# Thresholded attention and a maxout feed-forward on one core: another written order, other PSUM slots and other masks

## The chip, the core and the metric

The kernel runs on one core of a Trainium2 chip. The engines are TensorE (PE in the profile; PEld is its loading of weights), VectorE (DVE), ScalarE (ACT), GpSimd (POOL) and SyncE (SP), which here only issues transfers. Each takes its instructions strictly in the order in which they were written and waits on semaphores for the others. The metric is the device time of one execution in microseconds (us).

## The reference

```python
def _attn_ref(q, k, v, tau):                      # 8 batches, 8 heads, 576 positions, 64 wide
    scale = 1.0 / np.sqrt(q.shape[-1])
    scores = scale * np.matmul(q, k.transpose(0, 1, 3, 2))
    thresh = np.max(scores, axis=-1, keepdims=True) - tau
    scores = np.where(scores >= thresh, scores, -1000000000.0)
    scores = scores - np.max(scores, axis=-1, keepdims=True)
    attn = np.exp(scores)
    attn = attn / (np.sum(attn, axis=-1, keepdims=True) + 1e-09)
    return np.matmul(attn, v).astype(np.float32)

def _moe_ref(x, w1, w2, w3, w_out):               # 4608 tokens, 512 wide, 768 inside
    h = np.maximum(np.maximum(x @ w1, x @ w2), x @ w3)
    return (h @ w_out).astype(np.float32)
```

The heads of the first function, side by side, are the rows x of the second. All inputs and the output are float32.

## The kernel before

The work is cut into 16 quads: four heads of one batch. A quad has nine chunks, each with 128 rows of queries for two heads, so a chunk has two halves of scores, 128 x 576 each; there are 144 chunks and 288 halves. Two quads make a batch. When a batch's two quads are through, its feed-forward can run: 18 pieces that make the hidden rows (three weights by six blocks of 128) and then the output pieces.

A half goes through these steps. TensorE makes its scores in a PSUM slot (a bank of 1024 columns; there are four slots, 0 to 3). VectorE copies them to an SBUF tile z and takes the row's largest value on the way (`maximum`, line by line in the print below). ScalarE and VectorE then make the numerators and their sum. VectorE takes the reciprocals of a chunk's two sums, GpSimd multiplies them in (tile P, bfloat16), and SP turns P by a transposing transfer into the quad's tile ptq. Once all nine chunks of a quad are turned, TensorE multiplies them with v (two products to a quad), and ScalarE or VectorE evacuates the result to the feed-forward's input xt.

How a half's numerators are made is told by its digit in `MASKED`:

- 0, plain: VectorE computes a threshold th from the largest value, ScalarE applies a Prelu to z with it (values under the threshold become huge), and ScalarE takes the exponential and its sum.
- 1, masked: ScalarE takes the exponential of z, VectorE compares it with the smallest admitted numerator, multiplies and sums, in one instruction that reads z twice. There is no threshold and no second pass on ScalarE.
- 2, direct: as 0, but ScalarE reads the scores from the PSUM slot, not from z, and needs no separate threshold. The slot is free only when ScalarE has read it, and not already when VectorE has.
- 3: direct and masked.

Ahead of a quad's scores come transposes of its q and k on TensorE (T), which ScalarE and VectorE evacuate (tiles qt, kt) and of which GpSimd makes a copy with the halves of partitions swapped (qs). The weights come in twelve pieces through a staging tile and are cast to bfloat16 on GpSimd. 38 warming matmuls stand at the start.

What sets the order is the string `ORDER`: one letter for each step, read from left to right, and each step writes its instructions at the end of its engines' queues. S, T, O, F and N put work on TensorE into the PSUM slot whose digit follows (scores, transposes, product with v, feed-forward piece, last ninth of the output rows), and B is the second half of the oldest open F. The letters that follow them:

- m, s, e, n, k: a half's first pass on VectorE, its threshold, its first pass on ScalarE, its exponential on ScalarE (unmasked) or its masking on VectorE (masked)
- r, p, t: a chunk's reciprocals, the normalising of one half on GpSimd, the transposing transfer on SP
- a, c, q, y: evacuation of turned q and of turned k, the swapped copy, the cast of v
- h, v, u, w, x, j, f: evacuations of feed-forward pieces, output pieces and products
- l, g, z, o, i, d: a load of q, k or v, a load of weights, its cast, and the stores

All transfers stand in one queue, SP's, but for three at the start and two at the end, which ScalarE's queue issues.

Of the kernel before, what the change touches and what calls it, by code (L numbers as in the profile page):

```python
# [45 lines left out]
nyrrsmyBepT1svS0hpcT2nS3zmaS1erpgsF2mntpsBmnS3yvF1etssT0myeBprS2cnpS3mnS0ympelF2epF3lmBnzslssvS0htBrqmeS2vpn
S1gF0sepmF3teqBmF2erssvpBtnBkphF0eS1vtS3znmF2nrBmqteS1rpvBnS3pmlnF0pmgeS1qsBsrhmS3pevS2npS1mF0npsO3ermpesmO2
zewepgsskBxtT3nF1vS2nklBarS0mlphS3mtepF2sS1rmnyBmetF3pvT0eBpcnS2tzT1nvS0asmzS3temS2qeS1meF0trkpmS3lenpBmnlys
reklpF1umerpskS3upBeoketmS0uS2umpS3tesmS1qeT0myO2nqlrsnlprcO3etqsmepwS0xptS1mnF3psnmS2BlerskpS1thF0meF3pmeBF
2ktnBveBsrS1nvpS0hmyF3emF2npBrssT0eprtvBaF1kS3nqvBeF0myhyS2kyleF3mBelBvnpS2snsS0vptemS1pnF3rmpT2tnBmpeF0scS1  # L50
htBrnmpF3erT2rpvlBasS1pstvnS2pmeF0pS3emtBqnmT2S1hcqS3empF2eS0rsqmtS1epsmBeF3pmnF0stsvBeBknF2klhF1BvelS0nrvpB
emT3pS2arvS0ptnS3mpnO1smtesrkpeF2swnlrpmeT0S1qtescS3epBmnpmnT0trskS3paS1umS0ulqmeS3lmyS1nopS2smelS0rmeS3psmn
O1ypersmqO2etkpemO0lewqxlknpS3tS1keF2momS3lexF0ktT1enkBercpnsBpumN1ertkphkF3jS0rursS1empBnmF2ptS0vpS1smeF3yt
BsnsmBpnvS0pT1hmF2atT3srepS0cF1eprBsmeqF3vnByBynvplS2nsS0plmhS1mteS2mF0nF3mteS1rrspBnmS2pelvBlepF1smT0leqBvl
aS2rkhF3oqnsS0mtS1epmBeqsF2ssmtS0epvBeyF1mnF3vpBesrS0ktphBermS1npT2svO0nytmpncT3eS1wF2nrmS0aBrsmnqF3vnT1pS0c
eBptsF2mhpS1eS3pmteS0qmBeO1spmnkteF3rvnpT0BsskapS2xvS0erS1qmtnS3pmnF2mqlespmeS1rtkBepresmT3puS1cuS0ptmnS3pS2
meyS1lrekpF0tnsmempO3lekteskO2nrsmpeBkpxrnwS1uptS3muS2pnmF0yoeS1mF3lesymBtnS2srkpS1hmBeF0spveF2ertBmpT3nrsvS
1paBlmpnS0tS3qhmF1epsmS2leBymF3tevF0nBknlS1rsvpS2esmqnBF3srmhpS1epS0tmeF2pssBrempBtesvS0ynF1mT3lnpBvF0lhsrcS
2tnT1mBnF3valS2nrBsqmeF0pvS1epS2meBptsmS3eqF1hmT2peBcS3tnskT2O0arkplnmO2lerpvewptS3xkpS1nF2meF0sstreBsmpS3nv
pBnmS1tS2hmT3eF0rmpnF1cBpnBrevptT3S2apvS0qmtS3S1enmqF2esrsqmiepmleS0soykeS1plBnmemtS3ukS0uT1snrlO2cpekynO1me  # L60
ymeF3pwxskteS0keS1BrrnkopmF2pmS0BqeuurtsmF1phS3srnpS2meT0ptBmeS3ykpaN2esvempF0tS1jkpF3ermBeS2ptvnS1pmBnS0rls
hsmpS2elF3mqntS1mpF0nsrBskpeF2lsmBetBpveF1yhvS3lnkS2lesF0mytnBmBerqsS3veF2lpvnF1pBsmT0htBceF3rT2vnpBsaS0pvnF
1qmtS2nBsrnmT0pS3hrcpF2esS1mpteS0rmpS3emBpntF1svqnS0ssBmpeoT2vO3lamtneF1wS0nrlBpmeS3qsrS2hsmS0pnmF1eptS3smeB
pmF2ntS0veS3rsmnpS1BnpO0veytrempS2empS3xsmS1tekF0nsknlT2rmpBelmlpnscS3quS1umyS2eorT0kpeO3tmeyO1ewlepsmF3etka
rknS2qklT0nBmxespcS2eryF0mpF1uskpuBtnS2BhmqF3nsvS0peS2srmtpF1eBmpeF0srvnBptS2hyS3pmeF1lmeBlBevtF3nkT2S0arrvp
BnS2mphS1smpF0ntS3smnpBmeF1lsT2esvlF3nrBrcptBnvpS2eS0qmlhS1tsnprsmT3F2epmS0aptBemF3yevS1oS0nqmBnpsrS2mnF1ptv
S0epmBeS3mthS2skeF0F1snmlBeklO3ersvpnrmByepF0swT2eqtBvnqF3ssrcS1hpiBmpT0S2vaptS1snmS0pnT3mqF2tecT1BarmS3pnS1
vqeS0mF2pesrmnptmS3npT1seS0qctBeymqermpS1eS3mpuF0nmtuskS1eS2klnS3smBesrsepO1upmemO2txrkpukeO3wnkpS0xS2emF3et
rmS1pnBssspmF2hS0rtepS3mnBpmF1etS0veF3mnN2rnpBpjF0evtF2esBkBkhF1nsvS3eBmBevO3hrkS2pwnS1mnF3prmS2eptsF0mnBpsS
1sevyS2terBmpeF3svS1iyepBmoS0yhmtF2ekF3nBsmS1ersBvpnF0pmeF2BvteS1hBmF3rsS0vpeF1rknpBBmnO2vhptO0xrpnS3pwS2trm  # L70
# [759 lines left out]
```

## Time and profile before

| | |
|---|---|
| median of 3 runs | 446.71 us (445.96 to 448.13) |
| span of the profiled execution | 444.8 us, from its first to its last instruction |
| granted TensorE clock over the span | 0.988 |
| transfers | 88.50 MB, 199 GB/s over the span |
| HBM read and written | 35.65 MB and 9.44 MB |

The profile is of one execution. Its times count from the first instruction of the span; what lies around the span (the run's time minus it) is in the runs' times alone. All instructions go through one recording helper, so nearly all rows name line 93, and rows are told apart by their tiles: sc are scores, tp transposes, ph and po the two parts of the feed-forward, o the products, z the halves, ptq the turned P.

### The profile page before, as it was taken

How to read it: one execution, taken by the hardware profiler on the slowest of the kernel's cores; microseconds unless marked ns; L12 is line 12 of the kernel's file. 1: busy time of each engine (PE TensorE's matmuls, PEld its weight loads, DVE VectorE, ACT ScalarE, POOL GpSimd, SP SyncE). 2: the span in 40 equal slices, each digit the busy share in tenths (PEclk: the TensorE clock that was granted, in tenths of full speed). 3: DMA queues.
4: the chain of work that ended last, by engine and by line, in shares of the span. 5: the costliest groups of instructions: out<-in, count | busy, mean ns of one | idle time of the engine just before them, and what ended most of it. 6: DMA issues, size and time to landing. Idle time of an engine off the chain costs nothing.

```text
span 444.8 us, 14254 instructions
## 1 busy us (share of the span) xinstructions
PE 422.4 (95%) x5188; PEld 320.2 (72%) x5190; DVE 392.8 (88%) x1228; ACT 403.0 (91%) x836; POOL 311.9 (70%) x420
## 2 busy tenths in 40 slices
PE   7767789999999999999999999999999999999996
PEld 6334347787788767787788777788688886787873
DVE  3887999999999999999999999998999998899642
ACT  3999999999999999999999999899999999987632
POOL 2799989997878687696785877676676685457400
PEclk8998999999999999999999999999999999999999
DMA  7999999999999999699899999989999977487633
GB/s 188 275 293 199 291 169 269 235 243 262 229 180 194 212 222 292 125 256 167 143 234 189 230 198 203 209 168 210 208 206 194 244 151 105 83 179 136 145 116 108
DMA packets 213959, 88.50 MB, mean 199 GB/s; under 512 B 189184, under 2 KB 202240, under 8 KB 213888
## 3 DMA queue, kind: packets, MB, share of 16 engines
q1 hardware_dynamic: 213360, 86.96, 95.9%
q8 instruction: 41, 0.67, 0.6%
q10 hardware_dynamic: 528, 0.62, 0.5%
q14 instruction: 30, 0.25, 0.2%
HBM read 35.65 MB, written 9.44 MB: 101 GB/s over the span
## 4 chain that ended last, share of the span: by engine, by line
PE 86%; ACT 5%; DVE 4%; issue 2%; DMA 1%; SPq 0%; DVEq 0%; ACTq 0%
PE ph L93 32%; PE sc L93 32%; PE po L93 10%; PE o L93 9%; ACT z L93 5%; PE tp L93 3%; DVE z L93 3%; DMA qm<-in_q_dram 1%; ACT qt L93 1%; SPq L93 0%; DVE xt L93 0%; DVE hm L93 0%; DVE stage L93 0%; DVE rs L93 0%; ACT ob L93 0%
## 5 line engine op out<-in xcount | busy, mean ns | idle before, releaser
L93 POOL TENSOR_SCALAR P<-z,rs 128x576 bf16<-128x576 f32 x250 | 200.6, 814 | 63.3 <-DVE rs L93 28.1
L93 DVE TENSOR_SCALAR_CACHE_REDUCE z<-sc 128x576 f32<-128x576 f32 x250 | 183.7, 750 | 14.8 <-PE sc L93 10.1
L93 PE MATMUL sc<-kt,qs 64*128 64x256 f32 (+2 forms) x640 | 182.6, 423 | 5.7 <-DVE z L93 2.3
L93 PE MATMUL sc<-kt,qt 64*128 64x320 f32 (+2 forms) x640 | 182.4, 433 | 5.2 <-ACT z L93 3.3
L93 PE MATMUL ph<-xt,w 64*128 64x288 bf16 (+2 forms) x2160 | 170.8, 283 | 0.1
L93 PEld LDWEIGHTS <-w 64*128 64x128 bf16 (+1 forms) x2160 | 130.1, 94 | 28.6 <-issue 4.3
L93 ACT ACTIVATE z<-z 128x576 f32<-128x576 f32 x174 | 117.6, 679 | 0.1
L93 PEld LDWEIGHTS sc<-kt,qs 64*128 64x128 f32 (+1 forms) x640 | 92.4, 180 | 25.7 <-DVE z L93 5.7
L93 ACT ACTIVATE z<-z,th 128x576 f32<-128x576 f32 x143 | 106.2, 769 | 5.0 <-DVE th L93 4.2
L93 PEld LDWEIGHTS sc<-kt,qt 64*128 64x128 f32 (+1 forms) x640 | 91.9, 179 | 19.7 <-ACT z L93 5.9
L93 DVE SCALAR_TENSOR_TENSOR z<-z 128x576 f32<-128x576 f32 x76 | 62.2, 830 | 0.5 <-ACT z L93 0.5
L93 PE MATMUL po<-wo,hT 64*128 64x512 bf16 (+3 forms) x454 | 53.5, 354 | 0.3
L93 POOL COPY qs<-qt 64x640 f32<-64x640 f32 (+3 forms) x66 | 43.0, 652 | 10.8 <-ACT qt L93 7.2
L93 ACT ACTIVATE z<-z,nm 128x576 f32<-128x576 f32 x68 | 50.6, 767 | 0.0
L93 DVE TENSOR_TENSOR hm<-ph,hm 128x576 bf16<-128x576 f32 (+2 forms) x54 | 37.0, 686 | 9.2 <-PE ph L93 8.9
L93 ACT ACTIVATE hm<-ph 128x576 bf16<-128x576 f32 (+2 forms) x54 | 31.8, 589 | 13.4 <-PE ph L93 12.8
L93 POOL TENSOR_SCALAR P<-stage,rs 128x576 bf16<-128x576 f32 x38 | 30.4, 804 | 19.3 <-ACT z L93 5.4
L93 PEld LDWEIGHTS <-hT 64*128 64x128 bf16 (+2 forms) x456 | 30.0, 95 | 16.5 <-issue 2.3
L93 DVE TENSOR_TENSOR hT<-ph,hm 128x576 bf16<-128x576 f32 (+2 forms) x54 | 37.0, 686 | 4.0 <-PE ph L93 2.3
L93 PE MATMUL o<-ptq,vb 128*64 128x64 bf16 (+2 forms) x544 | 39.0, 281 | 0.0
L93 ACT ACTIVATION_READ_ACCUMULATOR z<-z 128x1 f32 x174 | 34.3, 197 | 0.0
L93 PEld LDWEIGHTS <-vb 128*64 128x64 bf16 x544 | 23.3, 111 | 12.8 <-issue 4.9
(45 smaller groups left out, 431.6 us busy)
## 6 DMA issues: line engine op xcount, KB each, us to landing
vm<-in_v_dram SPq DMA_DIRECT2D x32, 256.0 KB, 4.8
qm<-in_q_dram SPq DMA_DIRECT2D x15, 512.0 KB, 5.0
km<-in_k_dram SPq DMA_DIRECT2D x15, 512.0 KB, 5.3
out_dram<-ob SPq DMA_DIRECT2D x14, 512.0 KB, 4.0
stage<-in_moe_w_dram SPq DMA_DIRECT2D x9, 512.0 KB, 5.2
ptq<-P SPq DMA_TRANSPOSE x144, 4.0
vr<-in_v_dram SPq DMA_DIRECT2D x16, 128.0 KB, 3.4
stage<-in_moe_w_out_dram SPq DMA_DIRECT2D x3, 512.0 KB, 4.9
```

Source lines behind the costliest of these rows:

```text
L93: ins = fn(*a, **kw)
```

## The change

Two constants are replaced, `MASKED` and `ORDER`. No function, tile or pool differs. The 288 digits differ in 115 places; the string has 3481 characters where it had 3465, because it has 16 thresholds (s) more, and four n became k. All else in it occurs as often as before, at other places and with other slot digits.

```diff
 MASKED = """
-232222322322222222021032222202332122123122200200111000000000100000000011
-000010111020011000101000000001100001001000010011111100000000100100000000
-110010030111000100010000000001010100001110001011010100110000000000000000
-100101101011000000120000001010000000110011100000001110001000010011111021
+320220312002220000101010000320210002020210010010301000000010100000001101
+001001011010101100001000000000110000101010001111011000100000100010000000
+110001001110100100010000001000111000000100011011101000011000010000010000
+010101000111000100100000000101000000011110001110101000000000101000011121
 """
...
 ORDER = """
-llllllglllT0laclT1laclzllqqS0qqS1meS2mS3lmlT0enlkS1ylmlT2eamelrnpS3leqlmnyS1qcapS0emtnrcS3pmnT2qmepgrelS1qya
-gS0pmelT2mqnS3tcpemqS2nlkT1eytaS0rmnT1kpermS3yS2enczrmS1qT0enmepnqtS3nprmaymgpeS0lptS2mppT0mtpS1enencnqsS3re
...
+lllllllllT1lcaqqlT2S3agcqqmlS2S0elmlkeT1lmnS2lscS0aelrmS3plmeqmlqnS2zeslS1mT3nlpS0maygecreqekpS2nmnpT3meyskS
+2qaetqT0mnS1yrcnplT2rsmpS0elS3rpamemqnT1tpS2eclpnmS1persS2mnpS0tsmS1eqgmeqsnszS3nrT0mtpemlS1paS2smepT0mnqS1t
...
 """
```

The digits by kind, over all 288 halves and over the first 36 and the second 36:

| | plain (0) | masked (1) | direct (2) | both (3) |
|---|---|---|---|---|
| all, before | 169 | 78 | 33 | 8 |
| all, now | 185 | 86 | 13 | 4 |
| halves 1 to 36, before | 3 | 2 | 25 | 6 |
| halves 1 to 36, now | 18 | 5 | 10 | 3 |
| halves 37 to 72, before | 22 | 8 | 5 | 1 |
| halves 37 to 72, now | 24 | 9 | 2 | 1 |

SP at the very start of the program; stage is the staging tile of the weights, the other tiles are loads of q, k and v (q_147 and k_149 hold the ninth column of rows). Before:

```order
L93 DMA q_147<-in_q_dram 64x2x64
L93 DMA qm<-in_q_dram 64x512 x2
L93 DMA stage<-in_moe_w_dram 128x4x256
L93 DMA k_149<-in_k_dram 64x2x64
L93 DMA q_147<-in_q_dram 64x2x64
L93 DMA km<-in_k_dram 64x2x512
L93 DMA qm<-in_q_dram 64x2x512
L93 DMA vm<-in_v_dram 64x4x256 x2
```

Now:

```order
L93 DMA q_147<-in_q_dram 64x2x64
L93 DMA qm<-in_q_dram 64x512 x2
L93 DMA k_149<-in_k_dram 64x2x64
L93 DMA q_147<-in_q_dram 64x2x64
L93 DMA km<-in_k_dram 64x2x512
L93 DMA qm<-in_q_dram 64x2x512
L93 DMA vm<-in_v_dram 64x4x256
L93 DMA stage<-in_moe_w_dram 128x4x256
```

The first piece of the weights moved behind the other half of the first quad's q and k and half of its v.

ScalarE in the first quad; z<-sc,nm is a direct first pass, z<-z,th a plain one, z<-z,nm a masked one, z,sm<-z the exponential with its sum. Before:

```order
L93 ACTIVATE qt<-tp 128x2x320
L93 ACTIVATE z<-sc,nm 128x576 x2
L93 ACTIVATE z,sm<-z 128x576
L93 ACTIVATE z<-sc,nm 128x576
L93 ACTIVATE z,sm<-z 128x576 x2
L93 ACTIVATE z<-z,th 128x576
L93 ACTIVATE z<-sc,nm 128x576
L93 ACTIVATE z,sm<-z 128x576 x2
L93 ACTIVATE z<-z,nm 128x576
```

Now:

```order
L93 ACTIVATE z<-z,th 128x576 x2
L93 ACTIVATE z,sm<-z 128x576 x2
L93 ACTIVATE z<-z,th 128x576
L93 ACTIVATE qt<-tp 128x2x320
L93 ACTIVATE z<-z,th 128x576
L93 ACTIVATE z,sm<-z 128x576
L93 ACTIVATE z<-z,nm 128x576
L93 ACTIVATE z<-z,th 128x576
L93 ACTIVATE z,sm<-z 128x576
L93 ACTIVATE qt<-tp 128x2x256
```

Direct passes became plain ones, which wait for a threshold of VectorE, and the second evacuation of a turned q stands nearer to the first.

TensorE between the second and the third product of the first batch (the third is the first of the second quad; its instructions are o<-ptq). Before, from the stretch's first transposes to its last:

```order
L93 MATMUL tp<-identf,km 128x64 x8
L93 MATMUL tp<-identf,k_277 128x64 x2
L93 MATMUL sc<-kt,qs 128x320
L93 MATMUL sc<-kt,qt 128x256
L93 MATMUL sc<-kt,qs 128x256
L93 MATMUL sc<-kt,qt 128x320
L93 MATMUL tp<-identf,qm 128x64 x8
L93 MATMUL sc<-kt,qs 128x320
L93 MATMUL sc<-kt,qt 128x256 x2
L93 MATMUL sc<-kt,qs 128x320
L93 MATMUL tp<-identf,km 128x64 x8
L93 MATMUL sc<-kt,qt 128x320
```

Now, from the stretch's beginning:

```order
L93 MATMUL tp<-identf,km 128x64 x8
L93 MATMUL tp<-identf,k_305 128x64 x2
L93 MATMUL sc<-kt,qt 128x320
L93 MATMUL sc<-kt,qs 128x256
L93 MATMUL sc<-kt,qs 64x256 x2
L93 MATMUL sc<-kt,qt 64x320 x2
L93 MATMUL tp<-identf,qm 128x64 x8
L93 MATMUL sc<-kt,qt 64x320 x2
L93 MATMUL sc<-kt,qs 64x256 x2
L93 MATMUL sc<-kt,qs 128x256
L93 MATMUL sc<-kt,qt 128x320
```

Of the three groups of transposes there two are left; the third stands behind the products. In the whole stretch there are nine halves of scores, before and now.

Further on, SP's order differs in how far loads run ahead of the turned P: ahead of the 94th transposing transfer stand 83 of the 104 loads before and 93 now, and ahead of the 40th 49 and 51.

More of the change, by code (lines that the diff above doesn't have):

```diff
@@ L46 @@
[L46 to L70, printed above, removed]
@@ L71 @@
-npS0mnF3pmteF1pBeBvtS0rS2vpS3empF1ktkF0kBereskpemBkperumO2uptO3xpN1wtenkO2jrF3pxF1hpF2nvF3tvF1rhF2pvF3pvF1hF
-2tvF3vF1hF2voF3vF1ohF2vF3vF1hF2vO3vO1wF2xuuF1oF0hiF3vF1vF0hF3vF1vF0hF3vF1vF0hF3vF1vF0hF3vF1vF0huF3vF1ovF3uoF
-0uoN1fjdi
+lllllllllT1lcaqqlT2S3agcqqmlS2S0elmlkeT1lmnS2lscS0aelrmS3plmeqmlqnS2zeslS1mT3nlpS0maygecreqekpS2nmnpT3meyskS
+2qaetqT0mnS1yrcnplT2rsmpS0elS3rpamemqnT1tpS2eclpnmS1persS2mnpS0tsmS1eqgmeqsnszS3nrT0mtpemlS1paS2smepT0mnqS1t
+eT3rcplemqS0nS2tymanskS0yeS3srpetS1pnmgpekS2eqtsmnynrmpS0esklzT3emlnrcpnsrtS3permgpemepmtS0nzslnS1pmepkS2emt
@@ new lines @@
+nS0plmnresmpS2erspsS0mtepO3mleqklnT0perwntS2pnlS1zmasmepS0teS3qmnS2qrstnrS1mpeO3pnmtpemT2nprsS0ceytS1mnkpT0x
+stmeS3plesrS2mgpeS1slmpangkS2nrmS0petrmpS1emS3pelmO0qnsmpnO1serkpewS3etkS2qxT0lmnF1zsceF3smBepS0rkhpBemT2tS1
+apvS0nmqF3nF2trmyBzngssBveT0pS1shrcgpS3nmT2peF0mtpS1arseT2myS3pecF1nymBtnS2vpnS3rsmpS0etsmpBeF2mzntF3vBeyS0k
+yhgBrempS1nsF2vtpF0esmlBqesBrlvqnS3klF1phS2mleF0prsnsmBpS3tevBpnmF2nqS1vS3ezrmBnF0mptS1hsrspBlemS3gpevS2yeS1
+mF0tnmpO3nkzesmO2esrwpeBgkpxT3vF1aS2rkepBtmnS3lpsS0hmF2eqmS1eBytsrmyF3nzlvT0eT1cBpnS2tvpaS0nsrzmS1etmS3peS2m
@@ new lines @@
+pF0tskeqemF1nsrmpetBkpnkS3tukS2lumBelymlrS0rsuplS2umyS3lepmS1oepT0smO2nqmntyrO3cqelkpelwS0xS1pssmeF3pemS2F0n
+rmpBeskS1phBktF2evF3eBmnBvS0thrsS1kpnlF3mnlF2prBsmeByevtT0F1lavpS3eBpmnS2sF0srshmpF3ekBpnBtvnS2qrvS0eprmF3et
+S1mqnBlsmpT2hF0srcpeS1tyF3emplBnspT2vBapS1ssnvS2qemF0tqS3emBynmT2tS1hrcpS3empS0ntsF2melS1mF3nsBrmpntF0vpeBos
+BkeF2khF1tnsBveS0rvptBnmT3pS2avS0esqrmO1erpmteT3pwnS0pcF2epmntS3keT1lsS0rnmpBemptarskqS3usS1meS0ptmuS3nqmS1e
+lmpS2elS0srmpS3nlmpO1eosmqelO2kyxemO1nwterkpT0eS3ceF2pmnykyS0estrBkpxkelF1rmluS3pulskBnyN0lemhkS2ptjF3sermS1
@@ new lines @@
+peBmF2pnvS0npS1rsmBnptmF3eT0ssvBatS1khF2qlemS0BerrpmT1epF3svtF0nsqcBeS2pvnBtpmeS1oyrS3mhpS2nmptF1nsmS0pleBrm
+pF3nvS2teT0sslmF1eBkaBnsrqvS2hS0qmeF3ptmS1nBpsmnF2prevS0F1ptessmBpeBsvtF3hkS0lnBrmpleS1vT2peO0mnlscnT3lrwS1p
+aF2mepS0treBpmF3nvyT1qnBcS0hpF2srempS1teS3mqBnkS0ptnO1smemteF3rvxlT0BskaS2evqS1npmS0tnysS3meF2smpermqeT0S1sc
+pnBrmtepkyS0uS3muyS1epmS2lnF0pmoermpelS3skpO2elklnkO1elswnrmByxektpS1usrS3umS2peF0mpeS1mBynpsmtF3hS2srknpBtm
+eS1F0pveF2sntmBnT3rvpS1atBpmeS0yrS3shmqtS1essF2mpeF0kqnF3smBetBrpvnlBprevS1lphS2lmnS0pmF3eptrS1mnBpmnF0ptsS2
@@ new lines @@
+veBosmeF1svT3nBtrecpS2hF0pmtnF3skBeT1srvS2paBtemqF0lnvS1pS2emBqermS3pnF1smT2eBchS3lskeT2O0lkakeqO2mtnsqlvS3x
+wpS1nsrF2mpeF0rmpBestS3pevByemS1hS2tmpT3nF0rsmpnF1cBpeBtveT3S2rnvpS0astmpS1nmyS3eyF2smqnrstmepS1lnqS0mBelpsm
+elkT1uS0ceS3lmeO1rknpiO0ewpumtnF1kelkxS2lkeS3sBrmepntpmF0uorS2rpuBnmyS3hsF1tmepT2lBkapS0essvS3eN2pmtnrmpF0ek
+pS1jtBrnmF3lpnvS2opS1smeS0mBetS2mhS1ersmpF3tnF0kpBemF2sBrsevpBkF1qhtvS3nS2srpnrmBpeS0mF3pnmF2yteBvpeT0svqF1e
+tBsscF3hkBnT2vS0aBemlqS2nvpF0nT1rmpBesS3cphF2rsmtpeS1rS0pnmS3teqBmF1epsvS0ntpsBmelT2ymO3evntrspF1welS0kaBnmS
@@ new lines @@
+3qS2hmpS0nrsF1mqeS3smpF2eBtrsmpnBvnpS0sS3epmS1etrvO0pelmekS2yxtmS3eF0mnpmnyT1yssrkS2npBemtpeclS3urS2pmuS1nsm
+T0tO3akoeqO2elwpnlkT0eyrF3cximeqlS0snpBmeptskS1uF0mnBsurkpF1hrS2eBpmteS0pvF3lnS2prmeBpstF1mnF0peslvBkS2hS3rm
+peBtrF1epsmT2npvBtaF3kpS0nsvBtemqS2ohS1rymnpF0sS3metpBemT2nF1rscpF3evBtqnBsvpS2hsrS0pemS1npmF2temT3S0assBnmF
+3tnvS1S0ermpBemS2peF1svS0nmBerS3mpthS2kF0pnF1smeBrempO3nsvpteskF2qnBwBnrvtpT0eF3srscqS1hBepmT0S2vaS1smnqT3S0
+mtnqF2secT1yBparmS3eqvS1eS0mpeF2mpempT3nS1ctqnS0smBermtnpS3kepS1muF0usrskpeS3meS2tpmeS1oBknmemnO3kuurO2kyxeO
@@ L74 @@
+1wetpsnkpS0xS2meF1rmnS3pBrsptmS0hF2pemS3perF1smBptnsS0vpeF3ktN2emeskBjF0rnvptBersS2pohBpF1evpF3nmBtnBkO0hsvt
+eS2wrS1nrpmF3npsmS2eBpsmF1npvS0eytS2rsymBnpF3veipS0mBS1mhtF2nrsF3mpeBstpS1evF0emBeBvtS1hsF2nmS3nF0rsmpF1ekBp
+nBvBesvO2hO3rkxpntS1rweS0pmF3nmpS2F1spremBpteBvpS0eS2vtS3mF1metkeF0mnnBrkpekBukurO1upoO2xpO1wprN3xptuF2jpF1h
+F0tvF3vF1hF2vtF0vF1hF2vF0ovF1hF3vF2ivF1hF0vF2vF3hF0vO2vO3wF1xF0uF2hF3voF0vF2hF3vF1vF0hF2vF1vF0hF2vF1vF3hF2vF
+0vF1hF2vF0vF2uF1ouN2ofjdi
 """
```

3 lines of the change are left out of this document (removed).

## The prediction

> **What bounds the kernel now.** I read the page's busy shares first, then the chain of waits, then a table of busy time cut at every 36th first pass over a half of scores (the kernel does 288 of them, two to a chunk of 128 queries).
>
> ```profile
> span 444.8 us, 14254 instructions
> PE 422.4 (95%) x5188; PEld 320.2 (72%) x5190; DVE 392.8 (88%) x1228; ACT 403.0 (91%) x836; POOL 311.9 (70%) x420
> ...
> PE 86%; ACT 5%; DVE 4%; issue 2%; DMA 1%; SPq 0%; DVEq 0%; ACTq 0%
> ```
>
> ```profile
> core 0: us, PE busy (x) PEld busy (x) DVE busy (x) ACT busy (x) POOL busy (x), PEclk, DMA share, GB/s
> 8.90:53.30 44.40, 33.11 (x254) 18.74 (x252) 36.90 (x112) 42.14 (x93) 39.27 (x54) 0.90 1.14 264
> 53.30:99.00 45.70, 43.00 (x538) 31.65 (x540) 44.84 (x142) 45.45 (x96) 41.63 (x55) 1.00 1.11 230
> 99.00:148.00 49.00, 49.00 (x649) 39.87 (x647) 46.99 (x151) 48.79 (x101) 40.07 (x53) 1.00 1.13 217
> 148.00:201.50 53.50, 53.41 (x711) 40.23 (x706) 51.04 (x165) 52.16 (x108) 39.37 (x52) 1.00 1.04 221
> 201.50:250.60 49.10, 49.10 (x641) 38.24 (x637) 46.56 (x152) 47.98 (x100) 36.34 (x49) 1.00 1.05 190
> 250.60:305.30 54.70, 53.70 (x714) 42.62 (x709) 52.08 (x161) 52.14 (x109) 39.35 (x53) 1.00 1.00 199
> ```
>
> TensorE is idle for 444.8 - 422.4 = 22.4 us. The table says where: 11.3 us between 8.9 and 53.3, 2.7 us up to 99, then almost nothing but 1.0 us in the sixth row. The rest lies before 8.9 and in the store that ends the program. So from about 70 us on the end is the sum of TensorE's work, and both orders do the same work. In the first row ScalarE sets the pace (42.14 of 44.40); in the second ScalarE and VectorE both do (45.45 and 44.84 of 45.70). What TensorE gets done early is fixed by the order: the third product of the first batch stands behind the 52nd score half in both versions. A gain or loss is therefore a shift of that point, or a new stall behind it.
>
> **The change part by part.** Masks first. I count four kinds of half: plain (0), masked (1), direct (2), direct and masked (3). Direct falls from 41 to 17, masked rises from 86 to 90, plain from 169 to 185.
>
> ```profile
> L93 ACT ACTIVATE z<-z,th 128x576 f32<-128x576 f32 x143 | 106.2, 769 | 5.0 <-DVE th L93 4.2 <-DVE rs L93 0.4
> L93 ACT ACTIVATE z<-sc,nm 128x576 f32<-128x576 f32 x39 | 28.3, 746 | 2.9 <-DVE z L93 2.9
> L93 ACT ACTIVATE z<-z 128x576 f32<-128x576 f32 x174 | 117.6, 679 | 0.1
> L93 ACT ACTIVATION_READ_ACCUMULATOR z<-z 128x1 f32 x174 | 34.3, 197 | 0.0
> L93 DVE TENSOR_SCALAR th<-nm 128x1 f32<-128x1 f32 x169 | 22.7, 144 | 0.2
> L93 DVE SCALAR_TENSOR_TENSOR z<-z 128x576 f32<-128x576 f32 x76 | 62.2, 830 | 0.5 <-ACT z L93 0.5
> L93 DVE DVE_READ_ACCUMULATOR z<-z 128x1 f32 x76 | 6.1, 80 | 0.0
> L93 ACT ACTIVATE qt<-tp 128x640 f32<-128x640 f32 (+3 forms) x34 | 21.0, 618 | 4.5 <-PE tp L93 4.3
> ```
>
> A half that stops being direct costs ScalarE 769 - 746 = 23 ns, and VectorE a threshold of 0.144 us if it is plain. A masked half costs VectorE 0.83 + 0.08 = 0.91 us and spares ScalarE its exponential of 0.68 + 0.20 = 0.88 us. By blocks of 36 halves VectorE gains 15 thresholds = 2.2 us in the first, 2 thresholds and one masked half = 1.2 us in the second, then 0.1, 1.5 (two masked more, two thresholds fewer), 0.8 and 0.8 us. Against this stand its idle times in the table: 7.5, 0.9, 2.0, 2.5, 2.5 and 2.6 us. So I cost the first block and blocks three to six at nothing (VectorE's idle time hides them; without it they cost their 2.2 and 3.2 us), and the second at 1.2 - 0.9 = 0.3 us. Bounds: 0 and 1.2.
>
> The same stretch on ScalarE, up to the numerators of the second quad's last half: 38 exponents, 28 exponentials in both, 14 of the exponents direct where 32 were, and 9 evacuations of a transposed q where 8 were. That is 18 x 0.023 + 0.618 = 1.0 us more on the engine that sets the pace there. Bounds: 0 (if it hides in the 2.3 us that ScalarE idles) and 1.0.
>
> The start. SP now issues the first weight behind the first eight q, k and v loads, no longer ahead of the second half of q and k.
>
> ```profile
> 11.93 0.24 PE L93 MATMUL tp<-identf,qm 64*128 64x64 f32 x1 [0.48 <-DMA qm<-in_q_dram]
> 10.80 0.74 ACT L93 ACTIVATE z<-sc,nm 128x576 f32<-128x576 f32 x1 [0.39 <-DVE z L93]
> ```
>
> That q load is what ended TensorE's 0.48 us. ScalarE is nearly dense from 10.80 on, whoever waits for q, so at most 0.48 + 0.39 = 0.9 us comes back, at least nothing; I take 0.4 us, its own wait.
>
> The point where TensorE becomes dense. The last turned P of the second quad is issued at 65.4 and lands 3.5 us later, at 68.9; the product starts at 69.39.
>
> ```profile
> L93 SPq DMA_TRANSPOSE ptq<-P x1: 1504/1504/1504, 65.4 to 65.4; - x1
> ...
> DMA to landing us min/median/max: 3.5/3.5/3.5
> ```
>
> ```profile
> 69.39 1.18 PE L93 MATMUL o<-ptq,vb 128*64 128x512 bf16 x16
> ```
>
> ```profile
> 58.03 0.46 PE L93 MATMUL tp<-identf,qm 64*128 64x64 f32 x8 [0.64 <-DVE z L93]
> ```
>
> With +1.0 and -0.4 us the landing moves to 69.5. Between the second and third product TensorE has nine score halves as before, but two groups of transposes where it had three, so it would be ready 0.46 us sooner and stands until the landing. The start is 0.1 us later and the group is still to be done: 0.1 + 0.46 = 0.6 us. Bounds: -0.9 (the whole start gain, if the score halves ahead come sooner with it) and 0.5 + 0.46 = 1.0 (no start gain).
>
> The same look at the other late products:
>
> ```profile
> L93 SPq DMA_TRANSPOSE ptq<-P x1: 1398/1398/1398, 160.8 to 160.8; - x1
> ...
> DMA to landing us min/median/max: 3.4/3.4/3.4
> ```
>
> ```profile
> 164.42 1.18 PE L93 MATMUL o<-ptq,vb 128*64 128x512 bf16 x16
> ```
>
> The sixth quad's last P lands at 164.2, 0.2 us ahead of its product. Behind the last normalisation the new order leaves TensorE one group of transposes less before that product: 0.46 - 0.2 = 0.3 us of wait. Bounds: 0 and 0.5. The new order leaves more work there before the fourteenth quad's product and less before the tenth's and the twelfth's, but no product waited for a P in this trace; I take nothing there, with 0.5 us as the bound.
>
> Loads and stores. From the 40th turned P to about the 115th, SP issues up to ten loads earlier than it did.
>
> ```profile
> POOL vb L93 <- DMA vm<-in_v_dram: 3.2, 2, 2.6
> ...
> PE tp L93 <- DMA qm<-in_q_dram: 2.2, 3, 1.4
> ```
>
> No load after the first 12 us ended a wait of TensorE; GpSimd's 3.2 us lie on an engine idle 133 us. So earlier loads earn nothing in an execution like this one; if they had not been covered, the cost would have been these few us. A turned P now stands in SP's queue behind loads that it used to precede.
>
> ```profile
> 280.59 0.58 SPq L93 DMA_DIRECT2D km<-in_k_dram  x1
> ```
>
> ```profile
> SPq L93 <- POOL P L93: 130.9, 83, 6.0
> ```
>
> Each such load takes SP 0.58 us, but SP stands 130.9 us for P alone, which covers ten of them; I take nothing, with 0.58 us per turned P as the bound. The end is TensorE's alone: after the last scores come 33 us of matmuls without a gap, so softmax that ends sooner there earns nothing.
>
> ```profile
> 407.04 5.39 PE L93 MATMUL po<-wo,hT 64*128 64x512 bf16 x48
> ...
> 435.67 4.82 PE L93 MATMUL po<-wo,hT 128*128 128x512 bf16 x29
> ```
>
>
> One stall is left, and it shows what a masked half can do:
>
> ```profile
> 276.94 1.46 POOL L93 TENSOR_SCALAR P<-z,rs 128x576 bf16<-128x576 f32 x2
> ...
> 277.13 2.60 DVE L93 SCALAR_TENSOR_TENSOR z<-z 128x576 f32<-128x576 f32 x1
> ...
> 280.52 0.48 PE L93 MATMUL sc<-kt,qs 64*128 64x256 f32 x1 [0.94 <-DVE hm L93]
> ```
>
> ```profile
> L93 DVE SCALAR_TENSOR_TENSOR z<-z x76: 736/750/2601, 11.6 to 414.2; 128x576 f32<-128x576 f32 x76
> ```
>
> An operation with a median of 0.75 us took 2.60 while GpSimd normalised two halves of P in a row, and TensorE stood 0.94 us. That is one of 86 masked halves; with 90 I expect it again elsewhere, so 0. Bounds: -0.9 and +0.9. The Trainium skill, "SBUF — State Buffer", section "Who interferes with whom", says that a VectorE instruction with two SBUF inputs and a GpSimd instruction that reads SBUF exclude each other for a whole instruction, which speaks against each further masked half. The row agrees that it is held up, but by more than one GpSimd instruction. By that rule four more such instructions, each behind one normalisation, would add four normalisations to VectorE; by the mean of the row above they add a tenth of that, and the sum goes by the mean.
>
> Sum: 0.3 + 0.6 + 0.3 = 1.2 us on the span of 444.8. The median of the runs is 446.71, 1.9 us over that span; I carry this over: 446.71 + 1.2 = **447.9 us**.
>
> **The rivals.**
>
> VectorE becomes the bound: slower. The added 0.1 + 1.5 + 0.8 + 0.8 us of blocks three to six stop hiding, and the second block costs its full 1.2. It decides once VectorE has under about 1 us idle in a block, as it has in the second; the fourth would keep 1.0. Price: 3.2 + 0.9 = 4.1 us more, if half of it reaches TensorE 2.0: 450 to 452. For it: both engines at 95% to 98%, and the 0.94 us stall behind one long masked operation. Against: ScalarE is relieved in the same blocks by 0.88 us for each masked half, and so far TensorE stood still for almost none of VectorE's waits after 70 us.
>
> The change doesn't do what it says: slower too.
>
> ```profile
> DMA to landing us min/median/max: 3.2/4.0/8.1
> ```
>
> A turned P that lands in 8.1 us where 4.0 is the median is 4.1 late, and the tight products have 0.2 to 0.5 us. The new order is no looser there: from the last normalisation to the product it has no more work on TensorE for the second and sixth quads and less for the tenth and twelfth. One such landing costs 3.6 us: 451.5. For it: the three times shown differ by 2.2 us. Against: this profile holds the 8.1 and has no such stall.
>
> The head gains: faster. Direct halves keep a PSUM slot until ScalarE has read it, and TensorE waited for that:
>
> ```profile
> PE sc L93 <- ACT z L93: 4.0, 9, 0.7
> ...
> PE tp L93 <- ACT z L93: 2.9, 2, 2.1
> ```
>
> With 18 of 31 direct halves gone from the first block, these 6.9 us shrink, and ScalarE is fed sooner. It can win no more than its own idle time in the first row, 2.3 us; with the stall at 280 gone too that is 3.2: 443.5. Against: TensorE isn't the bound there, so most of its waiting moves only to another place.
>
> **How the numbers follow.** The forecast has 0.52; VectorE 0.22; a late landing 0.10; the head 0.16. By the bounds of its terms the forecast alone runs from 446.7 - 0.9 - 0.9 = 444.9 to 446.7 + 1.2 + 1.0 + 0.5 + 0.5 + 0.9 = 450.8. Half a per cent, 2.2 us, is about what a measurement of this kernel can tell from no change; 0.06 of the forecast's chance lies beyond it, past 448.9. So faster 0.16, same 0.46, slower 0.06 + 0.22 + 0.10 = 0.38. The range takes in the slower cases as far as 452 and the head's case down to 444.2; what is left out is most of that case and a tenth of the slower ones.
>
> **What would show it.** The first two rows of the table: if ScalarE's busy time up to the second quad's last landing grows by about 1 us and that product starts near 69.5 us plus or minus 0.5, the head is as I say; a start before 68.5 would be the third rival. VectorE's idle time in the second and fourth blocks, and TensorE's waits that it ends after 70 us, decide the first rival: under 1 us in all, it has fallen. A TensorE wait ended by a turned P in front of a product would be the second. If TensorE's busy time itself differs by more than 1 us, the premise of equal work is wrong, and with it the sum.

## The result, and the profile after

The changed kernel takes 443.85 us (median of 6 runs, 442.66 to 444.25), the kernel before 446.50 us (6 runs, 445.68 to 448.44): a ratio of 0.9939, 95% interval 0.9921 to 0.9958. It is 2.7 us faster. The forecast was 1.2 us slower.

The page of the changed kernel, with the span, the busy shares, the chain of waits, and the group of masking instructions:

```profile
span 442.0 us, 14289 instructions
PE 420.4 (95%) x5188; PEld 318.1 (72%) x5190; DVE 398.2 (90%) x1252; ACT 402.3 (91%) x828; POOL 319.5 (72%) x420
PE 84%; DVE 6%; ACT 5%; issue 2%; POOL 1%; DVEq 0%; POOLq 0%; ACTq 0%
L93 DVE SCALAR_TENSOR_TENSOR z<-z 128x576 f32<-128x576 f32 x80 | 67.2, 850 | 0.8 <-ACT z L93 0.8
```

VectorE does 5.4 us more than before (398.2 against 392.8) and GpSimd 7.6 us more, and the kernel is still faster. TensorE executes the same 5188 matmuls but is busy 2.0 us less (420.4 against 422.4). Equal work with unequal busy time is the sign that waits are counted inside "busy". Behind the seventh product with v (the next views say where that is) TensorE is busy 318.8 us before and 316.8 now, which is the whole 2.0; idle time makes another 0.9, about the one wait of 0.94 us that the prediction shows.

Where the time went is seen at points that stand behind equal work on TensorE in both orders: the starts of the products with v. Here are the 7th, 19th, 23rd and 25th, TensorE's instructions on tile o in a short window at each; the first of the two times behind the comma is the product's start. Before:

```profile
L93 PE MATMUL o<-ptq,vb x14: 190/376/383, 120.4 to 121.2; 128*64 128x512 bf16 x8, 128*64 128x64 bf16 x6
L93 PE MATMUL o<-ptq,vb x14: 190/376/383, 266.8 to 267.6; 128*64 128x512 bf16 x8, 128*64 128x64 bf16 x6
L93 PE MATMUL o<-ptq,vb x14: 193/382/404, 318.9 to 319.6; 128*64 128x512 bf16 x8, 128*64 128x64 bf16 x6
L93 PE MATMUL o<-ptq,vb x14: 192/382/403, 351.0 to 351.8; 128*64 128x512 bf16 x8, 128*64 128x64 bf16 x6
```

The changed kernel:

```profile
L93 PE MATMUL o<-ptq,vb x14: 192/382/403, 120.4 to 121.2; 128*64 128x512 bf16 x8, 128*64 128x64 bf16 x6
L93 PE MATMUL o<-ptq,vb x14: 190/377/383, 265.8 to 266.6; 128*64 128x512 bf16 x8, 128*64 128x64 bf16 x6
L93 PE MATMUL o<-ptq,vb x14: 192/382/403, 316.9 to 317.6; 128*64 128x512 bf16 x8, 128*64 128x64 bf16 x6
L93 PE MATMUL o<-ptq,vb x14: 191/378/403, 348.4 to 349.2; 128*64 128x512 bf16 x8, 128*64 128x64 bf16 x6
```

Up to 120.4 us nothing is gained. The whole 2.8 us of the span comes behind it: 1.0 us by the 19th product, 2.0 by the 23rd, 2.6 by the 25th. With the 15th product and the end added, and a second profile of each kernel (the experiments tell of those), the stretches in us are these; unrounded starts are subtracted:

| | 7th product at | to the 15th | to the 19th | to the 23rd | to the 25th | to the end | span |
|---|---|---|---|---|---|---|---|
| before | 120.4 | 99.0 | 47.4 | 52.1 | 32.2 | 93.8 | 444.8 |
| before, again | 120.8 | 102.8 | 47.4 | 52.1 | 32.2 | 93.8 | 449.1 |
| changed | 120.4 | 98.3 | 47.1 | 51.1 | 31.6 | 93.6 | 442.0 |
| changed, again | 121.9 | 98.3 | 47.1 | 51.1 | 31.5 | 93.6 | 443.5 |

The work between these points is equal: TensorE has the same numbers of score halves, transposes and feed-forward pieces ahead of each of these products in both orders. Two executions of one kernel agree to 0.1 us in every stretch but one (102.8, told below), so a difference of 0.3 us between the kernels is a property of the order. The head up to the 7th product varies by 1.5 us instead.

What the stretches lose can be read from the waits that TensorE and its weight loads have ahead of scores, from 120 us on. Columns: total us, times, longest. Before:

```profile
PEld sc L93 <- DVE z L93: 2.6, 10, 0.5
PEld sc L93 <- DVE hm L93: 2.0, 4, 1.3
PEld sc L93 <- ACT qt L93: 1.1, 5, 0.3
PE sc L93 <- DVE hm L93: 0.9, 1, 0.9
PEld sc L93 <- ACT hm L93: 0.9, 4, 0.3
PEld sc L93 <- DVE th L93: 0.8, 3, 0.4
```

The changed kernel, same window:

```profile
PEld sc L93 <- DVE z L93: 1.3, 5, 0.3
PEld sc L93 <- DVE th L93: 0.9, 3, 0.5
PEld sc L93 <- DVE stage L93: 0.8, 3, 0.4
PEld sc L93 <- DVE hT L93: 0.6, 2, 0.4
PEld sc L93 <- DVE hm L93: 0.6, 3, 0.3
PEld sc L93 <- ACT qt L93: 0.2, 1, 0.2
```

All such rows, shown or not, those ended by VectorE, ScalarE or GpSimd, sum to 10.9 us in 35 waits before (11.1 again) and to 6.0 in 24 in the changed kernel (6.9 again). The tile behind the arrow is that of the instruction that ended the wait; most often it is the instruction that empties the PSUM slot which the next scores want, or the one that holds it up on its engine. But for the two rows with 1.3 and 0.9 us as their longest, which belong to the one collision told of below, no wait is over 0.5 us. All but the 0.9 us are waits of weight loads (PEld), which run beside matmuls (38.24 us of them in the 49.10 us of the prediction's fifth row, in which PE is busy throughout), so the 4 to 5 us that are gone need not all be time; the time gained is 2.8 us. That these waits make the whole of it is argued from the rows and not shown wait by wait.

In the orders themselves the same is seen. Between the 8th product and the last scores, 43 of 198 score halves reuse a slot within six steps of the one that frees it in the old order, the nearest within three; in the new order 20, the nearest within five. The traces agree: behind 120 us, 30 score halves start less than 0.1 us after their slot's last reader ended (31 in the second execution), and 16 in the changed kernel (17). Where the scores start the moment the slot comes free, a delay of that reader can delay TensorE.

### The profile page after: what moved, and what is told of

The parts are those of the page before. It is cut to its first block, busy times and chain, and to the rows that moved or that the text cites. A ratio compares the mean times of both kernels' runs of the same rounds, so it can differ in the third digit from the quotient of the medians.

```text
span 442.0 us, 14289 instructions
## 1 busy us (share of the span) xinstructions
PE 420.4 (95%) x5188; PEld 318.1 (72%) x5190; DVE 398.2 (90%) x1252; ACT 402.3 (91%) x828; POOL 319.5 (72%) x420
## 4 chain that ended last, share of the span: by engine, by line
PE 84%; DVE 6%; ACT 5%; issue 2%; POOL 1%; DVEq 0%; POOLq 0%; ACTq 0%
PE ph L93 31%; PE sc L93 28%; PE po L93 10%; PE o L93 9%; ACT z L93 5%; DVE z L93 4%; PE tp L93 4%; PE warm L93 1%; POOL P L93 1%; DVE kt L93 1%; ACT qt L93 1%; DVE hm L93 0%; DVE stage L93 0%; DVE hT L93 0%; DVE th L93 0%
## 5 line engine op out<-in xcount | busy, mean ns | idle before, releaser
L93 PEld LDWEIGHTS <-w 64*128 64x128 bf16 (+1 forms) x2160 | 127.8, 94 | 32.2 <-issue 4.3
L93 ACT ACTIVATE z<-z,th 128x576 f32<-128x576 f32 x157 | 118.2, 770 | 1.7 <-DVE th L93 1.1
L93 ACT ACTIVATE z<-z 128x576 f32<-128x576 f32 x170 | 114.8, 678 | 0.3
L93 PEld LDWEIGHTS sc<-kt,qt 64*128 64x128 f32 (+1 forms) x640 | 93.2, 180 | 17.1 <-DVE z L93 5.2
L93 DVE SCALAR_TENSOR_TENSOR z<-z 128x576 f32<-128x576 f32 x80 | 67.2, 850 | 0.8 <-ACT z L93 0.8
L93 POOL COPY qs<-qt 64x640 f32<-64x640 f32 (+3 forms) x66 | 46.6, 705 | 23.0 <-ACT qt L93 19.7
L93 ACT ACTIVATE z<-z,nm 128x576 f32<-128x576 f32 x76 | 57.7, 767 | 1.1 <-DVE z L93 1.1
L93 DVE TENSOR_TENSOR hm<-ph,hm 128x576 bf16<-128x576 f32 (+2 forms) x54 | 37.0, 685 | 10.9 <-PE ph L93 10.0
L93 PEld LDWEIGHTS <-hT 64*128 64x128 bf16 (+2 forms) x456 | 28.4, 95 | 18.7 <-issue 2.2
L93 PE MATMUL o<-ptq,vb 128*64 128x512 bf16 (+2 forms) x544 | 38.7, 282 | 0.5 <-DVE z L93 0.5
```

Source lines behind the costliest of these rows:

```text
L93: ins = fn(*a, **kw)
```

## The experiments

Theory A, once the traces were read: the gain is in the stretch behind 120 us, by less of these short waits, and the collision at 277 us is the largest of them. The rivals are that the start brings it (B), that the masks carry it (C), that loads come in time (D), and that slots matter little by themselves (E, E2). All ratios are to the kernel before on the same chip, with the 95% interval.

**Half of the order.** h1 has the old order up to the 8th product and the new one behind it; h2 the other way round. The digits follow. From h1 against the kernel before:

```diff
-000010111020011000101000000001100001001000010011111100000000100100000000
+000010111020011000001000000000110000101010001111011000100000100010000000
```

> The old order up to the eighth product (120 us), the new order and its masks behind it. Theory A (the gain lies behind 120 us, in score halves of TensorE that wait less for PSUM slots): the whole gain, ratio to before 0.994, about 443.9 us. Rival B (the gain comes from the start, where a weight load moved and direct halves became plain): nothing, ratio 1.000, 446.5 us.

> The other way round: the new order up to the eighth product, the old behind it. Theory A: no gain, ratio 1.000, about 446.5 us. Rival B: the whole gain, 0.994, 443.9 us.

Measured: h1 0.9962 (0.9932 to 0.9991), h2 1.0021 (1.0001 to 1.0042). The gain follows the second half, and B, the whole gain from the start, falls. The traces say the same: the six profiles with the old start (two of before, h1, h5, x1, x2) reach the 7th product at 120.4 to 121.6 us, 120.9 in the mean, and the five with the new one (two of the changed kernel, h2, t1, t2) at 119.7 to 121.9, 121.0 in the mean. From the 19th product on h1's stretches are the changed kernel's (51.1, 31.6, 93.6), and its interval holds 0.994. But behind the join its profile takes 100.4 and 48.9 us, longer than either kernel; h2, joined at the same place, also takes 100.4, and 47.7, and then has the old 52.2, 32.2 and 93.8. Each of the two profiles is of one execution, 2.4 and 1.7 us above its kernel's median, so what a join costs by itself stays open.

**The masks alone.** The old order and its slots, with the new masks; 41 digits of the row below and 74 others change, and a threshold that the old order has no letter for stands right behind its first pass.

```diff
-232222322322222222021032222202332122123122200200111000000000100000000011
+320220312002220000101010000320210002020210010010301000000010100000001101
```

> The old order and slots with the new masks; a threshold that the old order lacks stands right behind its half's first pass. Theory A: the masks hardly change how long a slot is free before scores take it in the stretch after 120 us, so at most a third of the gain: 0.998 to 1.002, 445.6 to 447.4 us. Rival C (the masks carry it: less of ScalarE's time, slots freed by VectorE): 0.994 to 0.996, 443.9 to 444.7 us.

Measured: 1.0609 (1.0576 to 1.0643), outside everything expected. The table of busy time shows it in the stretch from 53.3 to 99 us, where TensorE had 43.00 before:

```profile
core 0: us, PE busy (x) PEld busy (x) DVE busy (x) ACT busy (x) POOL busy (x), PEclk, DMA share, GB/s
53.30:99.00 45.70, 37.60 (x411) 24.59 (x410) 36.94 (x119) 38.66 (x82) 32.45 (x43) 0.91 0.87 182
```

All engines are less busy there, the granted clock is 0.91 instead of 1.00, and behind the 7th product too the kernel takes 14.6 us more (339.0 against 324.4). Which half is masked and where its steps stand belong together; which of the thresholds it is was not tried. So this run is no test of C: it doesn't tell what the new masks give in the order that they were made for. What a single mask gives is told below.

**The loads.** h9 is the new order with its loads against the turned P where the old order has them (62 of 84 exactly, the others up to ten turned P sooner). h9b moves 50 of the 84 loads from the third quad on later, by 3.9 turned P in the mean over all 84 (6.5 over the 50), each at least 45 steps ahead of its first use. A piece of h9 (l is a load, t a turned P, p a normalising):

```diff
-2qaetqT0mnS1yrcnplT2rsmpS0elS3rpamemqnT1tpS2eclpnmS1persS2mnpS0tsmS1eqgmeqsnszS3nrT0mtpemlS1paS2smepT0mnqS1t
+qaellltqT0mnS1yrcnpT2rsmpS0eS3rpamemqnT1lltpS2ecpnmS1persS2mnpS0ltsmS1eqgmeqsnszS3nrT0mtpemS1paS2smepT0mnqS1
```

> The new order, but every load from the third quad on stands against the turned P where the old order has it (up to ten transfers later). Theory A: no load ended a wait of TensorE in either profile, so it keeps the gain: 0.994, 443.9 us. Rival D (the gain is in transfers that land in time): most of it is lost, 0.998 to 1.000, 445.6 to 446.5 us.

> The changed kernel with 50 of its 84 loads moved later, by 3.9 turned P in the mean and at most 14, toward where the old order has them (5.3 later), but each at least 45 steps ahead of its first use. Theory A: 0.993 to 0.995, no difference from the changed kernel. Rival D (the gain is that transfers are in time): 0.998 to 1.000, with waits on a load back in the trace.

Measured: h9 1.0665 (1.0628 to 1.0702), with this wait at the head of its list:

```profile
POOL vb L93 <- DMA vm<-in_v_dram: 33.5, 7, 9.7
```

That is no test of D: the new order also uses its loads sooner, so the old places are right in front of their uses. h9b was to mend that, and measured 1.0064 (1.0043 to 1.0085), against the expected 0.993 to 0.995. Its score waits are the changed kernel's (6.0 us in 23), and three stretches agree with it (98.2, 51.1 and 93.6); but it takes 48.7 us instead of 47.1 up to the 19th product, and 36.7 instead of 31.6 from the 23rd to the 25th, with this wait of a product and of its weight load:

```profile
PEld L93 <- DMA ptq<-P: 3.4, 1, 3.4
PE o L93 <- DMA ptq<-P: 3.1, 1, 3.1
```

The 24th product waited 3 us for a turned P; the other 2 us of that stretch were not followed up. In the other one a feed-forward piece waits 0.9 us for VectorE, at 227.8 us. So the places of the loads matter by over 1%, which I had not expected. It doesn't make D the cause of the gain: in the first profile of before no such wait stands behind 120 us, and the gain comes in stretches that repeat to 0.1 us. It says that the changed kernel needs its loads where they are.

**Each kernel a second time.**

> The changed kernel once more, to size the gain in the same runs as the next three and to have a second profile: ratio 0.994, and TensorE's excess time ahead of score halves behind 120 us about 3 us again, where the old order has 5.3.

> The kernel before, profiled a second time. Theory A: the score halves that start less than 0.1 us after their slot's release are about 30 of 191 again, and the waits ahead of score halves sum to about 5 us. If the vector operation of half 193 takes over 2 us again, its collision with GpSimd belongs to the old order; if it takes about 0.85 us, the 0.94 us wait behind it was of one execution.

The changed kernel measured 443.96 us, 0.9931 (0.9911 to 0.9951). The second profile of before has a span of 449.1 us, but repeats the collision, on VectorE at 281.4 us and on TensorE behind it:

```profile
281.40 2.59 DVE L93 SCALAR_TENSOR_TENSOR z<-z 128x576 f32<-128x576 f32 x1
...
284.78 0.48 PE L93 MATMUL sc<-kt,qs 64*128 64x256 f32 x1 [0.93 <-DVE hm L93]
```

2.59 us where the first execution had 2.60, and 0.93 where it had 0.94: it belongs to the order. So do the profiles of h2, s1 and x1 below, which keep that half masked in the old order: 2.55 to 2.66 us, and 1.00 to 1.02 us of wait. The waits that the two texts name (3, 5.3 and 5 us) are another measure than the rows' sums, which are 6.9 us for the new order and 11.1 for the old.

The 3.8 us that this execution loses between the 7th and the 15th product go back to a load of v that came late. GpSimd's cast stood for it, VectorE for the normalisation behind the cast, and TensorE's transposes for VectorE:

```profile
138.53 1.03 POOL L93 CAST vb<-vm 128x1024 bf16<-128x1024 f32 x1 [3.63 <-DMA vm<-in_v_dram]
...
140.31 0.76 DVE L93 TENSOR_SCALAR_CACHE_REDUCE z<-sc 128x576 f32<-128x576 f32 x1 [2.19 <-POOL P L93]
...
141.13 0.46 PE L93 MATMUL tp<-identf,km 64*128 64x64 f32 x8 [1.83 <-DVE z L93]
```

The runs of before on that chip lie between 445.83 and 450.93 us. Whether late loads make the upper ones, and whether the new order is looser there, was not settled. The median difference needs no such cause: the first profiles of the two kernels, without such a load, differ by 2.8 us, and the medians by 2.7.

**The slots made tighter.** The new order with other slot digits in the middle and nothing else: 48 of 198 score halves within six steps of their slot's release (t1), and 104 of 198 (t2), where the new order has 20. From t1:

```diff
-pF0tskeqemF1nsrmpetBkpnkS3tukS2lumBelymlrS0rsuplS2umyS3lepmS1oepT0smO2nqmntyrO3cqelkpelwS0xS1pssmeF3pemS2F0n
+pF0tskeqemF1nsrmpetBkpnkS3tukS2lumBelymlrS0rsuplS2umyS3lepmS1oepT0smO2nqmntyrO3cqelkpelwS0xS1pssmeF2pemS0F3n
```

> The changed kernel with other slot digits alone from the eighth product to the last scores, drawn so that score halves stand as close behind the step that frees their slot as in the old order (48 of 198 within six letters, the old order 43, the new one 20). Theory A (the gain is this margin): a third of the gain to all of it is lost, ratio 0.996 to 1.000. Rival E (margins of single slots don't count, the timing of the engines does): 0.993 to 0.995.

> The same with every slot taken from the youngest freed one that was freed at least four letters earlier (104 of 198 score halves within six letters). Theory A: more than the gain is lost, ratio 1.002 to 1.012. Rival E: 0.993 to 0.996.

Measured: 1.0235 (1.0209 to 1.0261) and 1.0439 (1.0413 to 1.0465), more than expected. The waits of t1 from 120 us on show it:

```profile
PEld sc L93 <- DVE z L93: 8.6, 19, 1.3
```

and of t2:

```profile
PEld sc L93 <- DVE z L93: 13.2, 37, 0.8
```

Summed as above, the waits ahead of scores are 19.6 and 29.4 us, 13 and 23 more than in the changed kernel; from the 7th product to the end t1 takes 13.8 us more. Against the changed kernel on the same chip (443.96 us) that is 3.1% and 5.1% by slot digits alone, with no instruction added: E falls. This shows what slots can cost, not yet that they are what the change gained. And the count is a poor measure of it: t1 has about as many near reuses as the old order (48 against 43) and is 2.4% slower than it. No wait in these rows is over 1.3 us, and TensorE still shows 94% busy in both.

**One half unmasked.** The old kernel with half 193 (counted from 0), whose masking took 2.60 us, made plain:

```diff
-110010030111000100010000000001010100001110001011010100110000000000000000
+110010030111000100010000000001010100001110001011000100110000000000000000
```

> The old kernel with one masked half made plain, the one whose masking took 2.60 us at 277 us and held TensorE for 0.94 us. If that meeting of VectorE and GpSimd comes in every execution: about 1 us faster, ratio 0.997 to 0.998. If it was one execution's chance: 1.000.

Measured: 0.9980 (0.9962 to 0.9997). From the 19th to the 23rd product its profile takes 51.1 us, as the changed kernel, against 52.1; the other stretches agree with those of before to 0.1 us, and the waits ahead of scores fall to 8.5 us. So the collision is worth 1.0 us, and it did not turn up elsewhere. (The half also gets its threshold, a letter s more, and an n for its k.)

**The slots chosen from the traces.** From the third product on each step gets the slot whose last reader ended earliest in the traces, in the old order (s1) and in the new (s2). From s1:

```diff
-mgntspcS2eqrseT3mtpeS0srmapS1mnT2ptS3mnqO0ceqmeO1prswnptnkS3pxS0meF1meS2zBresmT0qghF3klpF2nkBtaS1sveS0pemF3B
+mgntspcS2eqrseT3mtpeS0srmapS1mnT2ptS3mnqO0ceqmeO1prswnptnkS2pxS3meF0meS1zBresmT2qghF3klpF1nkBtaS0sveS2pemF3B
```

> The order and the masks of the kernel before; only the PSUM slot of a step is changed, from the third product on, to the slot whose last reader ended earliest in the trace of before (353 digits). Uses of score halves and first-pass pieces that start less than 0.1 us after their slot's release fall from 70 to 48 in that trace (46 in the trace of after). Theory A (the gain is short waits of TensorE for a slot, which the new order has fewer of): 0.994 to 0.998 of before. Rival E2 (the margins matter only together with the new order of the steps): 1.000 within 0.002. Slower than 1.002 would say that slots chosen from one trace don't carry over to the next execution.

> The order and the masks of the changed kernel; only PSUM slots are changed, in the same way, from the changed kernel's own two traces (342 digits; 46 tight uses become 40). Theory A: 0.990 to 0.994 of before, the lower end a little better than the changed kernel. Rival E2: as the changed kernel, 0.994. Above 0.996: the slots that the change brings are better than those chosen from traces.

Measured: s1 0.9998 (0.9979 to 1.0016), s2 0.9987 (0.9964 to 1.0010). Neither helps. The uses that start less than 0.1 us after their slot's release did become fewer in s1's own trace (behind 120 us, 47 score halves and first-pass pieces where before has 57), and the time did not follow: again the count is the wrong measure. By stretch s1 takes 99.3, 47.2, 52.3, 31.5 and 94.1 us: it has half of the changed kernel's gain between the 15th and the 19th product and all of it between the 23rd and the 25th, and gives it back elsewhere; one wait of 0.7 us, of a weight load at 177.7 us, is new. s2 loses 0.7 us between the 19th and the 23rd product and 1.5 us behind the 25th, with a wait of 1.2 us at an output piece at 409.8 us. A slot that is better for one step is worse for another.

**The slots where they gained, and the one mask.** x1 is the old kernel with s1's slots only from behind the 15th product to ahead of the 29th. x2 adds the unmasked half, here with a row of the slots:

```diff
-110010030111000100010000000001010100001110001011010100110000000000000000
+110010030111000100010000000001010100001110001011000100110000000000000000
...
-1paBlmpnS0tS3qhmF1epsmS2leBymF3tevF0nBknlS1rsvpS2esmqnBF3srmhpS1epS0tmeF2pssBrempBtesvS0ynF1mT3lnpBvF0lhsrcS
+1paBlmpnS0tS3qhmF1epsmS2leBymF0tevF3nBknlS2rsvpS1esmqnBF0srmhpS2epS3tmeF1pssBrempBtesvS2ynF3mT0lnpBvF2lhsrcS
```

> The order and the masks of the kernel before; the reassigned PSUM slots of s1_before_slots only from behind the 15th product to ahead of the 29th (153 digits in there; behind it the old slots under new numbers). Theory A (score halves' waits for slots, each at a fixed place): the stretch from the 15th to the 19th product takes 47.2 us instead of 47.5 and that from the 23rd to the 25th 31.5 instead of 32.1, the others as in the kernel before: 0.998 (0.9 us). Rival E2 (slots help only together with the new order of steps): 1.000.

> As x1_slots_where_they_gained, and half 193 without a mask as in h5_one_half_unmasked. Theory A: also the stretch from the 19th to the 23rd product at 51.1 us instead of 52.1, in all 1.8 us or 0.996, two thirds of the changed kernel's gain with the old order of steps. Rival E2: 0.998, as the one mask alone.

Measured: x1 0.9983 (0.9961 to 1.0005), x2 0.9949 (0.9919 to 0.9979). The starts of x2's 19th, 23rd and 25th product:

```profile
L93 PE MATMUL o<-ptq,vb x14: 190/376/383, 267.0 to 267.8; 128*64 128x512 bf16 x8, 128*64 128x64 bf16 x6
L93 PE MATMUL o<-ptq,vb x14: 192/382/403, 318.3 to 319.1; 128*64 128x512 bf16 x8, 128*64 128x64 bf16 x6
L93 PE MATMUL o<-ptq,vb x14: 192/382/404, 349.9 to 350.6; 128*64 128x512 bf16 x8, 128*64 128x64 bf16 x6
```

Its stretches are 99.0, 47.2, 51.4, 31.5 and 93.8 us. Beside before that is 0.2, 0.7 and 0.6 us less in the three middle ones, where the changed kernel gains 0.3, 1.0 and 0.6, and nothing in the other two, up to the 15th product, where nothing was changed, and behind the 25th. The old order of the steps thus gets 1.5 of the 2.8 us in its profile by one mask and some 150 slot digits (behind them the old slots are only renumbered); its waits ahead of scores are 7.4 us. x1 has the slots' part alone: 47.2 and 31.5 us, as s1 and x2, where both profiles of before have 47.4 and 32.2. By the stretches E2 falls; the ratios alone would hardly tell, since x1's interval holds 1.000 and x2's ends at 0.998. What the new order has beyond that, 0.7 us up to the 15th product, some 0.3 between the 19th and the 23rd and 0.2 behind the 25th, was not isolated. None of these kernels is faster than the changed one.

## Why the prediction was wrong

**The step that failed** is the one in the first part: "from about 70 us on the end is the sum of TensorE's work, and both orders do the same work". The work was the same; the sum of busy time was not the work. I took 49.10 of 49.10 us busy to mean that nothing can be gained, and so costed the middle at nothing. The text had said what would break this, TensorE's busy time differing by more than 1 us, and it differs by 2.0. What stood against it were the waits ahead of scores, which the prediction did not add up: the largest row behind 120 us is 2.6 us of ten pieces, all of them together are 10.9 us, and the new order has 6.0.

**The stall at 280 us** had the right rows and the wrong value: "with 90 I expect it again elsewhere, so 0", with -0.9 as the bound. It was the bound. One long operation ahead of one slot was a place in the order, not a rate per masked half. The kernel with that half unmasked showed 1.0 us for it. Beside the long masking, from 277.13 to 279.73 us, GpSimd ran three normalisations in a row and not two; the third has a row of its own, because its half lies in a staging tile:

```profile
278.38 0.74 POOL L93 TENSOR_SCALAR P<-stage,rs 128x576 bf16<-128x576 f32 x1
```

The masking ended 0.6 us after the third, so it may have stood for all three; that is read from the times and was not tested. VectorE's masking did get slower in the new order: 80 by 850 ns less 76 by 830 is 4.9 us, 1.9 more than four instructions at the median of 0.75. That is six times the 0.3 us that the mean gave. The Trainium skill's rule in "SBUF — State Buffer", section "Who interferes with whom", gave an estimate of four normalisations, some 3.2 us at the rows' 0.8. That lies above what is measured. No wait of TensorE for it shows: the longest maskings of the changed kernel take 1.62 and 1.58 us, and behind 70 us its matmuls wait for VectorE once, 0.2 us.

**VectorE's second block (+0.3)** and the first rival. The masks came as counted, and VectorE's idle time shrank in the third and the fifth block (the rows are cut at the same first passes, not at equal work of TensorE):

```profile
core 0: us, PE busy (x) PEld busy (x) DVE busy (x) ACT busy (x) POOL busy (x), PEclk, DMA share, GB/s
8.70:51.60 42.90, 31.48 (x252) 20.42 (x252) 37.77 (x125) 41.27 (x88) 37.04 (x50) 0.88 1.08 252
51.60:98.70 47.10, 43.50 (x543) 32.29 (x541) 44.94 (x147) 46.98 (x101) 44.06 (x58) 1.00 1.16 240
98.70:148.20 49.50, 49.15 (x648) 36.45 (x646) 48.70 (x155) 47.45 (x96) 42.58 (x53) 1.00 1.17 246
148.20:201.20 53.00, 52.93 (x711) 40.93 (x706) 51.99 (x167) 52.45 (x109) 40.63 (x52) 1.00 1.13 213
201.20:250.30 49.10, 49.10 (x649) 38.52 (x647) 48.35 (x153) 48.69 (x99) 37.19 (x51) 1.00 1.09 219
```

In the second block 2.2 us of VectorE's idle time are left, where the prediction had it used up, so nothing of the +0.3 is seen. 0.8 us are left in the third block and 0.75 in the fifth, under the 1 us at which I let the rival decide, and 1.0 in the fourth; yet TensorE is idle 0.35 us in the third and not at all in the fifth. By the other sign, TensorE's waits for VectorE behind 70 us, the rival has fallen for the matmuls (0.2 us, where it was 0.9); the weight loads still wait for VectorE for about 8 us, where it was 9. A threshold of idle time per block didn't tell whether one engine holds up another. The chain does show VectorE's share up from 4% to 6%.

**The third product (+0.6).** Predicted at 69.5 plus or minus 0.5 us, it starts at 68.81, under that and above the 68.5 that would have spoken for the third rival. ScalarE's busy time in the first two rows grew by 0.7 us (88.25 against 87.59) and not by 1.0, the landing came sooner and not later: the last transfer was issued at 64.1 and took 3.3 us, so P was there at 67.4, 1.5 us earlier than before. And the landing no longer ended the wait:

```profile
L93 SPq DMA_TRANSPOSE ptq<-P x2: 1302/1304/1305, 62.7 to 64.1; - x2
...
DMA to landing us min/median/max: 3.2/3.3/3.3
```

```profile
65.98 0.48 PE L93 MATMUL sc<-kt,qs 64*128 64x256 f32 x1 [1.02 <-DVE z L93]
...
68.81 1.22 PE L93 MATMUL o<-ptq,vb 128*64 128x512 bf16 x15 [0.18 <-DVE z L93]
```

TensorE came late from its own score halves. The 0.6 us gained up to here (69.39 before) are gone by the 7th product (120.4 in both), so the head's net is nothing: term and third rival were both wrong about the place. A single start says little here, though: in the second executions this product starts at 70.19 in the changed kernel and at 69.86 before.

**The sixth quad (+0.3).** I misread the row. The product at 164.42 us is the tenth, the fifth quad's second; with two to a quad, the sixth quad's first is the eleventh, which started at 165.7 and had 1.4 us of slack, not 0.2. In the changed kernel the tenth and the eleventh start at these times, without a wait:

```profile
164.67 1.18 PE L93 MATMUL o<-ptq,vb 128*64 128x512 bf16 x16
...
165.91 0.40 PE L93 MATMUL o<-ptq,vb 128*64 128x512 bf16 x2
```

Its last P landed at 164.0. The term was never there.

**Loads and the tail at nothing** came out so: the changed kernel has no TensorE wait on a transfer behind 120 us, and from the 25th product to the end it gains 0.2 us. But the reason, that nothing waited for a load in the one profile I had, was weak: the second execution of before loses 3.8 us to one, and moving 50 loads later, by 6.5 turned P in the mean, cost the changed kernel over 1%.

**The second rival** didn't occur; no product waited for a P. **The third rival's** time, 443.5, was nearly right by luck: its place was wrong but for the stall at 280, since h2 and the 7th product's starts show that the head doesn't bring the gain.
